# Sorting the value rows of later batches: one full-array matmul per 512 columns, or sixteen 32 by 32 array tiles per 384

## The chip, the cores and the metric

The kernel runs on one core of a Trainium2 chip. The metric is the device time of one execution in microseconds; a profiled execution has in addition a span, from its first to its last instruction, and a trace of every instruction on the five engines: TensorE (PE, with its weight loads as PEld), VectorE (DVE), ScalarE (ACT), GpSimd (POOL) and SyncE (SP), which issues transfers.

## The reference

Attention over blocks that are first mixed by a doubly normalised matrix, and then a two-layer network with a squared relu. The shapes: 4 batches, 8 heads, 768 positions in 8 blocks of 96, head dimension 64; the network goes from 512 to 2048 and back for 3072 tokens.

```python
P = sort_net                                  # (4, 8, 8, 8)
for _ in range(5):
    P = np.exp(P - np.max(P, axis=-1, keepdims=True))
    P = P / (np.sum(P, axis=-1, keepdims=True) + 1e-09)
    P = P / (np.sum(P, axis=-2, keepdims=True) + 1e-09)
k_sorted = np.einsum('bhij,bhjcd->bhicd', P, k_b)
v_sorted = np.einsum('bhij,bhjcd->bhicd', P, v_b)
scores = scale * np.matmul(q_b, k_sb.transpose(0, 1, 2, 4, 3))   # within a block
attn = softmax(scores)
x = np.matmul(attn, v_sb)                     # to (3072, 512)
h = x @ w_in
out = (s * np.maximum(h, 0.0) ** 2 + b) @ w_out
```

## The kernel before

Everything is in bfloat16 with 32-bit sums. A raw tile of keys or values of one batch has 128 partitions and 48 x 64 columns. The partition is (head, block j, half z of the block), and a head is (a, e): pair a of four, member e of two. The column is (c, d): position c in the half block, and head dimension d.

Sorting mixes the blocks of a head: a sum over j. `build_pd` turns a batch's mixing matrix into a 128 by 128 weight `PD[b]` that is zero wherever the heads or the halves differ, so that one matmul over all 128 partitions sorts all heads at once. Its columns are (e, z, a, i), i being the new block.

The work of batch b is written out by hand into slots of the network of the batch before. `ffn1(t, slots)` is the first layer of half batch t: eight times two groups of four matmuls (tile `hps`, line 473), a relu on ScalarE (line 485), a square on VectorE (line 486), and after group i the pieces listed under slot i. `ffn2(t, slots)` is the second layer (tile `ops`, line 497), three output tiles of sixteen matmuls with a store each (`store`, lines 522 and 525), and a slot after every four matmuls. Each engine works through its instructions in the order written.

For b from 1 to 3, with n = b + 1, the loop at the end of the kernel issues the loads of keys and query rows of batch n on the GpSimd queue (`load`, `load_q_rows`), then `ffn1(2b)`, `ffn1(2b + 1)`, `ffn2(2b)` and `ffn2(2b + 1)`. The slots of the first of these, `u0`, sort the values of batch n; those of `ffn2(2b)` sort its keys (`k_pairs`, tile `tpp`); those of `ffn2(2b + 1)` hold its scores (`s_piece`, tile `sc`), products (`p_piece`, tile `pv`), the transposes of its result (`t_dma`) and `build_pd` for the batch after. So the sorting of values that the change touches runs twice, for batches 2 and 3. Batch 1's values go another way (`v_piece`, tile `tv`), batch 0's too.

Values of batches 2 and 3 so far:

- `v_rows(n, u)`, slots 0 to 5: one matmul of 512 columns of the raw tile with `PD[n]` (line 347, tile `tvr`), and a VectorE copy back over the columns that were read (line 349).
- `v_back(n)`, slot 5: the sorted tile has the new block in its partitions, and the products want the position there. So it goes to DRAM in two transfers of 64 partitions on the sync queue (line 354), and back in four (line 358) into `VS`, whose partitions are (z, c) and whose columns are head and block. Each of the four reads what one of the two wrote.
- `q_dma(n)` (QD), slot 5 behind it on the same queue: two transposing transfers of the query rows (line 456).
- `load("v", n + 1, ...)` (LV), where a further batch follows: a one-column copy on GpSimd that waits for the transposed queries (line 90), and six loads (line 93).

The PSUM tiles come from two pools. `psa`, tag "a", has three buffers of two banks, used in turn by `hps`, `sc`, `pv` and the key sorting. `psb`, tag "b", has two buffers of one bank, used in turn by `ops`, `tvr` and others. A tile that takes a buffer waits until the one before it there has been read.

The script's order of the slots before:

```python
u0 = {i: [VRW(n, i)] for i in range(6)}
u0[5] += [VB(n), QD(n)]
```

Of the kernel before, what the change touches and what calls it, by code (L numbers as in the profile page):

```python
# [9 lines left out]
FP = mybir.dt.float32  # L10
BF = mybir.dt.bfloat16
AF = mybir.ActivationFunctionType
ALU = mybir.AluOpType
AX = mybir.AxisListType


def spread(t, dims):

    return bass.AP(tensor=t.tensor, offset=t.offset, ap=[list(t.ap[0])] + dims)
# [3 lines left out]
def kernel(  # L23
# [12 lines left out]
    nc = tc.nc  # L36

    B, H, S, D = q.shape
    NB = sort_net.shape[-1]
    BLK = S // NB  # L40
    BH = B * H
    NHP = H // 2
# [3 lines left out]
    HB = NB // 2  # L46
    TG = HB * BLK
    C2 = BLK // 2
    GAP = 64
    KR = GAP + C2  # L50
    NG = NHP * NB
# [5 lines left out]
    raw = [t.rearrange("b h (j z c) d -> b (h j z) (c d)", j=NB, z=2) for t in (q, k, v)]  # L57

    const = ctx.enter_context(tc.tile_pool(name="const", bufs=1))
# [7 lines left out]
    drp = ctx.enter_context(tc.tile_pool(name="drp", bufs=1, space=bass.MemoryType.DRAM))  # L67
    osb = ctx.enter_context(tc.tile_pool(name="osb", bufs=3))
    psa = ctx.enter_context(tc.tile_pool(name="psa", bufs=3, space=bass.MemoryType.PSUM))
    psb = ctx.enter_context(tc.tile_pool(name="psb", bufs=2, space=bass.MemoryType.PSUM))  # L70
# [9 lines left out]
    for c in range(0, C2, CV):  # L80
        nc.sync.dma_start(out=v0f[:, c:c + CV, :].rearrange("p c d -> p (c d)"),
                          in_=raw[2][0][:, c * D:(c + CV) * D])

    RAW = {}
# [36 lines left out]
    VS = [const.tile([KR, 2 * NG, VW], BF, name=f"vs{i}") for i in range(2)]  # L121
# [63 lines left out]
    nc.vector.memset(eps, 1e-9)  # L185
    jsel = const.tile([128, NB], FP)
    bm = const.tile([128, 2 * 2 * NHP], FP)
    idv = ident.rearrange("p (a e j z) -> p a e j z", a=NHP, e=2, j=NB)

    def permute(eng, b, src, cs=slice(0, C2), ds=slice(0, D)):  # L190
# [15 lines left out]
    def q_banks(b, half, engs):  # L206
# [3 lines left out]
        for u in range(2):  # L210
            tr = psb.tile([128, 1024], BF, tag="b", name="tqb")
            for a in range(2 * u, 2 * u + 2):
                for c in range(CQ):
                    for e in range(2):
# [9 lines left out]
            out=jsel, in_=ident.rearrange("p (h j z) -> p j h z", h=H, j=NB), axis=AX.XY, op=ALU.add),  # L224
        lambda: nc.vector.tensor_reduce(
            out=bm.rearrange("p (e z a) -> p e z a", e=2, z=2),
            in_=idv.rearrange("p a e j z -> p e z a j"), axis=AX.X, op=ALU.add),
# [3 lines left out]
                            op=ALU.subtract)  # L231
# [3 lines left out]
    for it in range(5):  # L235
# [8 lines left out]
        if it == 4:  # L244
            break
        nc.vector.tensor_reduce(out=rstat, in_=sn.rearrange("p i j -> p j i"),
                                axis=AX.X, op=ALU.add)
        if it == 0:
# [2 lines left out]
        nc.vector.tensor_tensor(out=sn, in0=sn, in1=spread(rrec, [[0, NB], list(rrec.ap[1])]),  # L251
                                op=ALU.mult)
    PD = {}
    later = const.tile([128, 2, B // 2, NB * NB], FP)

    def spread_rows(b, o):
# [14 lines left out]
    def build_pd(b, rows):  # L271
        tmp = rtp.tile([128, NB, NB], FP, tag="tmp", name="tmp")
        nc.vector.tensor_tensor(out=tmp, in0=rows.rearrange("p (i j) -> p i j", j=NB),
                                in1=spread(jsel, [[0, NB], list(jsel.ap[1])]), op=ALU.mult)
        pt = rtp.tile([128, NB], FP, tag="pt", name="pt")
        nc.vector.tensor_reduce(out=pt, in_=tmp, axis=AX.X, op=ALU.add)
        cs = rtp.tile([128, 1], FP, tag="cs", name="cs")
        nc.vector.tensor_reduce(out=cs, in_=pt, axis=AX.X, op=ALU.add)
        rc = rtp.tile([128, 1], FP, tag="rc", name="rc")
        nc.vector.reciprocal(out=rc, in_=cs)  # L280
        pd = const.tile([128, 2, 2, NG], BF, name=f"pd{b}")
        nc.vector.scalar_tensor_tensor(
            out=pd.rearrange("p e z (a i) -> p (e z a) i", i=NB),
            in0=spread(bm, [list(bm.ap[1]), [0, NB]]), scalar=rc,
            in1=spread(pt, [[0, 4 * NHP], list(pt.ap[1])]), op0=ALU.mult, op1=ALU.mult)
        PD[b] = pd

    def k_piece(b, c0, eng):
        ps = psa.tile([128, CK, 2, NG], FP, tag="a", name="tp")
# [50 lines left out]
        half(0, eng)  # L340
        return lambda eng: half(1, eng)

    def v_rows(b, u):
        w = 512 // D
        r = RAW["v", b][:, u * w:(u + 1) * w, :].rearrange("p c d -> p (c d)")
        ps = psb.tile([128, 512], FP, tag="b", name="tvr")
        nc.tensor.matmul(out=ps, lhsT=PD[b].rearrange("p e z g -> p (e z g)"), rhs=r,  # L347
                         start=True, stop=True)
        nc.vector.tensor_copy(out=r, in_=ps)  # L349

    def v_back(b):
        vd = drp.tile([2, 2, NG, C2, D], BF, tag="vd", name="vd")
        for e in range(2):
            nc.sync.dma_start(out=vd[e].rearrange("z g c d -> (z g) (c d)"),
                              in_=RAW["v", b][e * 64:(e + 1) * 64].rearrange("p c d -> p (c d)"))
        for e in range(2):
            for z in range(2):
                nc.sync.dma_start(
                    out=VS[b % 2][z * GAP:z * GAP + C2, e * NG:(e + 1) * NG, 0:D],
                    in_=vd[e, z].rearrange("g c d -> c g d"))  # L360

    AT = {}
    X = {}
# [42 lines left out]
        AT[b, half, hp] = at  # L406

    def p_piece(b, half, hp, fill=0):
        g0 = hp * NB + half * HB
        atf = AT.pop((b, half, hp)).rearrange("p e t -> p (e t)")  # L410
        if hp == 0:
            X[b, half] = xp.tile([BLK, HB, d_model], BF, tag="x", name="x")
        x = X[b, half]
        pv = psa.tile([128, 2, 512], FP, tag="a", name="pv")
        for i in range(fill):
            nc.tensor.matmul(out=pv[:, i % 2, 272:512], lhsT=zeros[:, 0:128], rhs=zeros[:, 0:240],  # L416
                             start=True, stop=True)
        for e in range(2):
            for n in range(HB):
                c0 = (e * HB + n) * BLK  # L420
                m = 128 if c0 + 128 <= 2 * TG else BLK
                nc.tensor.matmul(out=pv[0:m, e, n * VW:(n + 1) * VW],  # L422
                                 lhsT=atf[:, c0:c0 + m], rhs=VS[b % 2][:, e * NG + g0 + n, :],
                                 start=True, stop=True)
        pvv = pv[0:BLK, :, 0:HB * VW].rearrange("p e (n w) -> p e n w", w=VW)
        rec = rtp.tile([BLK, 2, HB], FP, tag="rec", name="rec")
        nc.vector.reciprocal(out=rec, in_=pvv[:, :, :, D])  # L427
        nc.vector.tensor_tensor(  # L428
            out=x[:, :, hp * 128:(hp + 1) * 128].rearrange("p n (e d) -> p e n d", e=2),
            in0=pvv[:, :, :, 0:D],  # L430
            in1=rec.unsqueeze(3).broadcast_to([BLK, 2, HB, D]), op=ALU.mult)
# [160 lines left out]
    def SC(b, h, i): return lambda: s_piece(b, h, i)  # L592
    def P(b, h, i): return lambda: p_piece(b, h, i)
    def TP(b, h, i, eng): return lambda: t_piece(b, h, i, eng)
    def VRW(b, u): return lambda: v_rows(b, u)
    def VB(b): return lambda: v_back(b)
    def TD(b, h): return lambda: t_dma(b, h)
    def PDB(b): return lambda: build_pd(b, later[:, b % 2, b // 2, :])
    def QD(b): return lambda: q_dma(b)
    def LV(b): return lambda: load("v", b, 6, QT[b - 1][:, NB - 1, 0, 0:1])  # L600
# [39 lines left out]
    for b in range(1, B):  # L640
        n = b + 1
        s0, s1, u0, u1 = {}, {}, {}, {}
        if n < B:
            load("k", n, 6, XT[2 * b + 1][:, HB - 1, NHP - 1, 0:1])
            load_q_rows(n)
            s0, s1 = halves(n)
            u0 = {i: [VRW(n, i)] for i in range(6)}
            u0[5] += [VB(n), QD(n)]
            if n + 1 < B:
                u0[5] += [LV(n + 1)]  # L650
        ffn1(2 * b, u0)
        ffn1(2 * b + 1, u1)
        ffn2(2 * b, s0)
        ffn2(2 * b + 1, s1)
# [30 lines left out]
```

## Time and profile before

| | before |
|---|---|
| median of 3 runs | 222.98 us (222.55, 222.98, 224.73) |
| profiled execution, its own time | 222.54 us |
| its span | 220.4 us |
| granted TensorE clock | 0.999 |
| PE / DVE / ACT / POOL busy | 213.6 / 126.0 / 109.4 / 70.8 us |
| first layer, line 473 | 512 matmuls |
| second layer, line 497 | 350 matmuls recorded |
| old sorting of values, line 347 | 12 matmuls of 512 columns |

The views used below: the page gives busy times and the share of each engine in the chain that ended last. The chain can also be read in order of time; there a row gives the time that a piece of work holds the chain, which for matmuls that follow one another is their pitch and not the longer duration of a single one. The groups of instructions by line give the mean duration of each shape. The timeline gives single instructions, with what ended the idle time ahead of them in square brackets. Lines with SPq show when the sync queue issues a transfer and how long the issue takes.

### The profile page before, as it was taken

What the parts mean: (1) busy time and instruction counts of PE and PEld (TensorE: products, weight loads), DVE (VectorE), ACT (ScalarE), POOL (GpSimd) and SP (SyncE); (2) the same over time, 40 slices, a digit from 0 to 9 for tenths busy, and PEclk for the clock granted to TensorE, in tenths of its full rate; (3) what the DMA queues carried; (4) which work ended last, traced back from release to release, by engine and by line L of the source; (5) the groups of instructions that cost most, each with busy time, mean ns of one, the idle gap of its engine ahead of it and who ended that gap; (6) DMA issues with size and microseconds to landing.
All of it is one profiled execution on the core that took longest, in us unless ns stands there. A gap on an engine that the chain in (4) does not pass through costs nothing.

```text
span 220.4 us, 5172 instructions
## 1 busy us (share of the span) xinstructions
PE 213.6 (97%) x2156; PEld 128.8 (58%) x2175; DVE 126.0 (57%) x257; ACT 109.4 (50%) x149; POOL 70.8 (32%) x127
## 2 busy tenths in 40 slices
PE   7989999999999999999999999999999999999994
PEld 5877766555465555666446555665446566654454
DVE  6777457567875768547636677547417744441222
ACT  4677687658635445664622535665424356550000
POOL 7659781689832004920050008800000000000000
PEclk9999999999999999999999999999999999999999
DMA  6999999999979662999979846999911940001212
GB/s 154 284 164 125 120 170 204 204 172 134 128 215 181 49 187 41 178 208 121 141 204 175 107 135 88 208 179 102 215 72 48 123 119 3 0 0 48 93 53 95
DMA packets 67255, 28.92 MB, mean 131 GB/s; under 512 B 51872, under 2 KB 63264, under 8 KB 67232
## 3 DMA queue, kind: packets, MB, share of 16 engines
q0 software_dynamic: 31168, 12.85, 49.5%
q1 hardware_dynamic: 36064, 15.74, 35.6%
q8 instruction: 17, 0.28, 0.6%
q14 instruction: 6, 0.05, 0.1%
HBM read 28.85 MB, written 7.86 MB: 167 GB/s over the span
## 4 chain that ended last, share of the span: by engine, by line
PE 90%; DMA 5%; DVE 1%; issue 1%; POOL 1%; ACT 0%; POOLq 0%
PE hps L473 38%; PE ops L497 36%; DMA rawk<-in_k_dram 5%; PE pv L422 4%; PE sc L380 3%; PE tpp L302 2%; PE ops L514 2%; PE tv L328 2%; PE tvr L347 1%; DVE vs L204 1%; PE tr L439 1%; PE scb L398 1%; POOL rawk L93 0%; PE sc L257 0%; PE pv L416 0%
## 5 line engine op out<-in xcount | busy, mean ns | idle before, releaser
L473 PE MATMUL hps<-xt,wi 128*128 128x384 bf16 x512 | 87.9, 326 | 0.0
L497 PE MATMUL ops<-wo,gt 128*128 128x512 bf16 x350 | 82.4, 379 | 1.4 <-issue 0.6
L485 ACT ACTIVATE rt<-hps 128x768 bf16<-128x768 f32 x64 | 51.8, 811 | 39.5 <-PE hps L473 38.3
L473 PEld LDWEIGHTS <-wi 128*128 128x128 bf16 x512 | 49.0, 98 | 32.6 <-issue 0.4
L486 DVE TENSOR_TENSOR gt<-rt 128x768 bf16<-128x768 bf16 x64 | 36.0, 565 | 41.2 <-ACT rt L485 41.0
L497 PEld LDWEIGHTS <-gt 128*128 128x128 bf16 x368 | 34.1, 98 | 37.4
L522 DVE SCALAR_TENSOR_TENSOR ot<-ops,s_bc,bias 128x512 f32<-128x512 f32 (+2 forms) x27 | 18.6, 691 | 34.7 <-PE ops L497 31.6
L388 ACT ACTIVATE at<-sc 112x768 bf16<-112x768 f32 x24 | 18.1, 808 | 30.1 <-PE sc L380 30.1
L428 DVE TENSOR_TENSOR x<-pv,rec 96x512 bf16<-96x512 f32 x32 | 22.0, 686 | 1.1
L115 POOL DMA_DIRECT2D qtok<-in_q_dram x24 | 18.6, 808 | 0.7 <-issue 0.7
L422 PEld LDWEIGHTS <-at 112*128 112x128 bf16 (+1 forms) x256 | 12.9, 101 | 6.7 <-ACT at L388 1.0
L202 ACT CAST ks<-tpp 64x512 bf16<-64x512 f32 x18 | 13.2, 731 | 4.7 <-DVE ks L204 4.1
L140 POOL DMA_DIRECT2D wi<-in_moe_w_in_dram x24 | 12.8, 558 | 5.5 <-DMA rawk<-in_k_dram 3.2
L422 PE MATMUL pv<-vs,at 112*128 112x66 bf16 (+1 forms) x256 | 13.9, 195 | 0.1
L204 DVE CAST ks<-tpp 64x512 bf16<-64x512 f32 x18 | 13.1, 729 | 0.9 <-ACT ks L202 0.5
L93 POOL DMA_DIRECT2D rawk<-in_k_dram x21 | 11.2, 550 | 2.7 <-issue 1.9
L93 POOL DMA_DIRECT2D rawv<-in_v_dram x18 | 9.7, 558 | 6.0 <-DMA wo<-in_moe_w_out_dram 4.6
L130 PE MATMUL z<-zeros 128*64 128x96 bf16 (+2 forms) x129 | 9.8, 241 | 1.3 <-DVE zeros L118 1.2
L90 POOL COPY rawk<-xt 128x1 bf16<-128x1 bf16 x2 | 0.4, 190 | 32.8 <-DMA xt<-x 32.8
L427 DVE RECIPROCAL rec<-pv 96x8 f32<-96x8 f32 x32 | 6.4, 200 | 6.4 <-PE pv L422 6.4
L130 PEld LDWEIGHTS <-zeros 128*64 128x64 bf16 (+1 forms) x130 | 7.5, 115 | 3.0 <-DVE zeros L118 1.2
L349 DVE CAST rawv<-tvr 128x512 bf16<-128x512 f32 x12 | 8.2, 683 | 0.0
(93 smaller groups left out, 137.9 us busy)
## 6 DMA issues: line engine op xcount, KB each, us to landing
out_dram<-ot SPq DMA_DIRECT2D x22, 256.0 KB, 2.6
rawv<-in_v_dram POOLq DMA_DIRECT2D x18, 128.0 KB, 5.3
rawk<-in_k_dram POOLq DMA_DIRECT2D x18, 128.0 KB, 4.1
qtok<-in_q_dram POOLq DMA_DIRECT2D x24, 96.0 KB, 6.5
wo<-in_moe_w_out_dram POOLq DMA_DIRECT2D x4, 512.0 KB, 10.8
v0f<-in_v_dram SPq DMA_DIRECT2D x4, 384.0 KB, 5.9
vd<-rawv SPq DMA_DIRECT2D x4, 384.0 KB, 6.4
vs<-vd SPq DMA_DIRECT2D x8, 192.0 KB, 8.1
```

Of the source, the lines that this page charges most:

```text
L93: nc.gpsimd.dma_start(out=ti[:, c:c + n, :].rearrange("p c d -> p (c d)"), in_=raw["qkv".index(t)][b][:, c * D:(c + n) * D])
L115: nc.gpsimd.dma_start(out=QTOK[b][:, n], in_=qv[:, n])
L130: nc.tensor.matmul(out=z[0:m, 0:w], lhsT=zeros[:, 0:m], rhs=zeros[:, 0:w], start=True, stop=True)
L204: nc.vector.tensor_copy(out=out, in_=in_)
L388: nc.scalar.activation(out=at, in_=sc[0:KR, :, 0:TG], func=AF.Exp, scale=scale)
L422: nc.tensor.matmul(out=pv[0:m, e, n * VW:(n + 1) * VW], lhsT=atf[:, c0:c0 + m], rhs=VS[b % 2][:, e * NG + g0 + n, :], start=True, stop=True)
L428: nc.vector.tensor_tensor(out=x[:, :, hp * 128:(hp + 1) * 128].rearrange("p n (e d) -> p e n d", e=2), in0=pvv[:, :, :, 0:D], in1=rec.unsq ...
L473: nc.tensor.matmul(out=H1[t, i][:, f, 0:TG], lhsT=wi[:, hp, fc:fc + 128], rhs=XT[t][:, :, hp, :], start=(hp == 0), stop=(hp == NHP - 1))
L485: nc.scalar.activation(out=rt, in_=h, func=AF.Relu)
L486: nc.vector.tensor_tensor(out=gt[:, 2 * i:2 * i + 2, :], in0=rt, in1=rt, op=ALU.mult)
L497: nc.tensor.matmul(out=ops, lhsT=gt[:, f, m * 128:(m + 1) * 128], rhs=wo[:, f, :], start=(f == 0), stop=(f == NF - 1))
L522: nc.vector.scalar_tensor_tensor(out=ot[:, ns], in0=ops, scalar=s_bc, in1=BIAS[0][:, ns], op0=ALU.mult, op1=ALU.add)
```

## The change

The sum over j stays within a head, and with (a, e, j, z) as the partition a head pair is 32 partitions. The changed kernel builds for batches 2 and 3 a second weight `PW[b]` with only 32 columns (z, e, i) beside `PD[b]`, from a mask `bmz` that is made once. A pair's 32 rows are one row group of the array.

`v_tiles(b, r)` takes the place of three `v_rows`. It has two rounds, r = 0 and 1, in slots 0 and 2. The raw tile's 3072 columns are eight stretches of 384, and round r takes the stretches 2c + r. For each c from 0 to 3 and each pair a there is one matmul of 32 rows and 32 columns: row group a, column group c, 384 columns of data, into PSUM bank a, partitions 32c onward. The four banks are one "a" tile and both "b" tiles. VectorE copies two banks at once and one more by itself, and ScalarE copies one.

The sorted tile now has (c, z, e, i) in its partitions and (a, r, x) in its columns. `v_back` sends it to DRAM in four transfers of 32 partitions and reads it back in two, one for each z. In `VS` the order of blocks and pairs changes, which `p_piece` follows in its index. `VB`, `QD` and `LV` move from slot 5 to slot 2.

```diff
+    bmz = const.tile([128, 2 * 2], FP)
...
         PD[b] = pd
+        if b >= 2:
+            if b == 2:
+                nc.vector.tensor_reduce(out=bmz.rearrange("p (z e) -> p z e", z=2),
+                                        in_=bm.rearrange("p (e z a) -> p z e a", e=2, z=2),
+                                        axis=AX.X, op=ALU.add)
+            pw = const.tile([128, 2 * 2 * NB], BF, name=f"pw{b}")
+            nc.vector.scalar_tensor_tensor(
+                out=pw.rearrange("p (x i) -> p x i", i=NB),
+                in0=spread(bmz, [list(bmz.ap[1]), [0, NB]]), scalar=rc,
+                in1=spread(pt, [[0, 4], list(pt.ap[1])]), op0=ALU.mult, op1=ALU.mult)
+            PW[b] = pw
...
-    def v_rows(b, u):
...
+    NC = C2 // 8
+
+    def v_tiles(b, r):
+        w = NC * D
+        raw = RAW["v", b].rearrange("p c d -> p (c d)")
+        two = psa.tile([128, 2, 512], FP, tag="a", name="tvr")
+        one = [psb.tile([128, 512], FP, tag="b", name="tvs") for _ in range(2)]
+        bank = [two[:, 0], two[:, 1], one[0], one[1]]
+        for c in range(4):
+            for a in range(NHP):
+                pr = slice(a * 32, (a + 1) * 32)
+                c0 = (2 * c + r) * w
+                nc.tensor.matmul(out=bank[a][c * 32:(c + 1) * 32, 0:w], lhsT=PW[b][pr, :],
+                                 rhs=raw[pr, c0:c0 + w], start=True, stop=True,
+                                 tile_position=(a * 32, c * 32))
+        v4 = raw.rearrange("p (a r x) -> p a r x", a=NHP, r=2)
+        nc.vector.tensor_copy(out=v4[:, 0:2, r], in_=two[:, :, 0:w])
+        nc.scalar.copy(out=v4[:, 2, r], in_=one[0][:, 0:w])
+        nc.vector.tensor_copy(out=v4[:, 3, r], in_=one[1][:, 0:w])

     def v_back(b):
-        vd = drp.tile([2, 2, NG, C2, D], BF, tag="vd", name="vd")
-        for e in range(2):
...
+        w = 2 * NC * D
+        vd = drp.tile([2 * 2 * NB, NHP, 4, w], BF, tag="vd", name="vd")
+        for c in range(4):
+            nc.sync.dma_start(out=vd[:, :, c],
+                              in_=RAW["v", b][c * 32:(c + 1) * 32].rearrange(
+                                  "p (a x) d -> p a (x d)", a=NHP))
+        for z in range(2):
+            nc.sync.dma_start(
+                out=VS[b % 2][z * GAP:z * GAP + C2, :, 0:D],
+                in_=vd[z * 2 * NB:(z + 1) * 2 * NB].rearrange("i a c (y d) -> (c y) (i a) d", d=D))
...
-        g0 = hp * NB + half * HB
+        def g(n):
+            i = half * HB + n
+            return i * NHP + hp if b in PW else hp * NB + i
...
-            u0 = {i: [VRW(n, i)] for i in range(6)}
-            u0[5] += [VB(n), QD(n)]
+            u0 = {0: [VT(n, 0)], 2: [VT(n, 1), VB(n), QD(n)]}
             if n + 1 < B:
-                u0[5] += [LV(n + 1)]
+                u0[2] += [LV(n + 1)]
```

More of the change, by code (lines that the diff above doesn't have):

```diff
@@ L253 @@
     PD = {}
+    PW = {}
     later = const.tile([128, 2, B // 2, NB * NB], FP)
@@ L286, in build_pd @@
         PD[b] = pd
+        if b >= 2:
+            if b == 2:
+                nc.vector.tensor_reduce(out=bmz.rearrange("p (z e) -> p z e", z=2), in_=bm.rearrange("p (e z a) -> p z e a", e=2, z=2),
+                                        axis=AX.X, op=ALU.add)
[5 more added lines that the diff above has]
+            PW[b] = pw
     def k_piece(b, c0, eng):
@@ L341, in v_piece @@
         return lambda eng: half(1, eng)
-    def v_rows(b, u):
[L344 to L349, printed above, removed]
-    def v_back(b):
-        vd = drp.tile([2, 2, NG, C2, D], BF, tag="vd", name="vd")
-        for e in range(2):
[L354 to L360, printed above, removed]
+    NC = C2 // 8
@@ L422, in p_piece @@
                 nc.tensor.matmul(out=pv[0:m, e, n * VW:(n + 1) * VW],
-                                 lhsT=atf[:, c0:c0 + m], rhs=VS[b % 2][:, e * NG + g0 + n, :],
+                                 lhsT=atf[:, c0:c0 + m], rhs=VS[b % 2][:, e * NG + g(n), :],
                                  start=True, stop=True)
@@ L594, in TP, with VT @@
     def TP(b, h, i, eng): return lambda: t_piece(b, h, i, eng)
-    def VRW(b, u): return lambda: v_rows(b, u)
+    def VT(b, r): return lambda: v_tiles(b, r)
     def VB(b): return lambda: v_back(b)
```

## The prediction

> **What bounds the kernel now.** I read the page first: which engine fills the span, which engine the chain that ended last runs through, and whether the matmul clock is full.
>
> ```profile
> PE 213.6 (97%) x2156; PEld 128.8 (58%) x2175; DVE 126.0 (57%) x257; ACT 109.4 (50%) x149; POOL 70.8 (32%) x127
> PEclk9999999999999999999999999999999999999999
> PE 90%; DMA 5%; DVE 1%; issue 1%; POOL 1%; ACT 0%; POOLq 0%
> ```
>
> TensorE (PE) is busy for 97% of the span, carries 90% of the chain, and its clock is full throughout. So a change matters through the time it gives TensorE or takes from it, or through a wait that it puts in front of a matmul. The second view is the chain in order of time around the code that changes, for batch 2, whose value rows are sorted during the first input layer of batch 1 (columns: start us, us, what; the DMA in the page's chain is its first row here, long before the change).
>
> ```profile
> 3.18 11.13 DMA rawk<-in_k_dram
> ...
> 78.87 1.30 PE hps L473 x8
> 80.17 0.22 PE tvr L347
> 80.39 1.30 PE hps L473 x8
> 81.69 0.22 PE tvr L347
> ...
> 87.75 0.22 PE tvr L347
> ```
>
> Here TensorE never waits. Eight matmuls of the input layer take 1.30 us, then one sorting matmul of 512 columns stands in the chain with 0.22 us. From 80.17 to 80.39 and from 81.69 to 81.90, by the next slot's start, it is 0.217 us, six times: 1.30 us a batch. Batch 3 does the same (twelve such matmuls in all), so 2.60 us of the chain belong to the old sorting. That is the most that could be won.
>
> **The change, part by part.**
>
> *Matmuls on the chain.* Removed: 12 matmuls of 512 columns, 2.60 us. Added: four rounds (two for each of batches 2 and 3) of 16 matmuls, each on a 32 by 32 piece of the array with 384 columns. No row shows such a piece, but the chain has smaller splits, each an excursion from full-array work and back:
>
> ```profile
> 26.10 0.88 PE tqb L216 x48
> 28.70 0.28 PE scb L398 x8
> 45.09 0.98 PE cps L576 x16
> 60.04 1.64 PE tv L328 x96
> 64.38 0.62 PE tv L328 x32
> 113.53 0.45 PE sc L380 x16
> 175.92 20.80 PE hps L473 x128
> ```
>
> hps is whole-array: 20.80 / 128 = 162.5 ns for 384 columns, so 384 columns at 2.4 a ns (160 ns) and 2.5 ns beside. The two tv rows differ by 64 matmuls and 1.02 us: 15.9 ns for 64 columns, where a lone one would need 64 / 2.4 + 2.5 = 29.2 ns. The pieces of 64 array columns therefore run two at a time (14.6 ns) with little lost. What is left, 1.64 - 96 x 15.9 = 0.11 us, is the price of leaving the full array and coming back. cps has four pieces of 32 array columns and 512 columns of data: 16 x (213.3 + 2.5) / 4 = 0.86 us, and 0.98 was measured: again 0.12 over. sc has two row halves: eight more matmuls cost 0.45 - 0.28 = 0.17 us, or 21 ns each, where two at a time gives (40 + 2.5) / 2 = 21.3; over: 0.11. So a round costs 0.115 us plus its matmuls divided by how many run at once. Four column pieces are shown, two row pieces too; both axes together by four are not.
>
> With all 16 at once the stream lasts 162.5 ns, and the round 0.28 us if they start together: the lower bound. The upper bound takes the closest spacing of starts that any row shows, 15.9 ns: 15 x 15.9 + 162.5 + 115 = 0.52 us. That spacing is already explained by the streaming of pairs, so the true spacing should be smaller; I take the middle, 0.40 us. Four rounds: 1.60 us (1.12 to 2.06). Against 2.60 us the gain is **1.0 us** (0.54 to 1.48).
>
> The Trainium skill speaks to this on both sides. "TensorE: Matmul & The Clock Gate", Part 3, gives about 4 ns between the starts of packed pieces; an estimate by that page is 60 + 162.5 + 115 = 0.34 us a round, a gain of 1.25 us. The same page, under "Wait — 56ns, not 53.3ns?", says starts never come closer than about 25 ns; the tv rows with 15.9 ns contradict it for pieces of 64 columns, yet if it held for 32 by 32 pieces it would cancel the change (first rival).
>
> *Evacuation.* Removed: 12 VectorE copies. Added per round: a VectorE copy of 768 columns, one of 384, and a ScalarE copy of 384. The rows for VectorE (L204) and ScalarE (L202) on PSUM tiles, columns as in the costliest groups:
>
> ```profile
> L204 DVE CAST ks<-tp 128x1024 bf16<-128x1024 f32 x1 | 1.2, 1223 | 0.3 <-PE tp L292 0.3
> L204 DVE CAST ks<-tkb 128x512 bf16<-128x512 f32 x1 | 0.7, 681 | 0.0
> L202 ACT CAST ks<-tp 128x1024 bf16<-128x1024 f32 x1 | 1.0, 1013 | 0.3 <-PE tp L292 0.3
> L202 ACT CAST ks<-tkb 128x512 bf16<-128x512 f32 x1 | 0.6, 592 | 0.0
> L349 DVE CAST rawv<-tvr 128x512 bf16<-128x512 f32 x12 | 8.2, 683 | 0.0
> 80.21 0.81 ACT L485 ACTIVATE rt<-hps 128x768 bf16<-128x768 f32 x1 [2.27 <-PE hps L473]
> 81.05 0.56 DVE L486 TENSOR_TENSOR gt<-rt 128x768 bf16<-128x768 bf16 x1 [0.83 <-ACT rt L485]
> 81.72 0.81 ACT L485 ACTIVATE rt<-hps 128x768 bf16<-128x768 f32 x1 [0.70 <-PE hps L473]
> ```
>
> Interpolated: 0.95 us for 768 columns on VectorE (0.68 to 1.22), 0.55 for 384 (0 to 0.68), 0.49 on ScalarE (0 to 0.59). Per batch VectorE does 2 x 1.5 = 3.0 us in place of 6 x 0.68 = 4.1. ScalarE's new 0.49 us fits in the 0.70 us for which it waits for the next hps. What could reach TensorE is the buffer of the second round. The first round runs 80.17 to 80.57; the relu ends at 81.02 and its square on VectorE at 81.61; the wide copy ends at 82.57 and the narrow one at 83.15. TensorE does two hps groups from 80.57 and asks for the same three buffers at 83.17. The last is free 0.02 us before, so it fits by a hair: a semaphore's delay may hold the fourth matmul a few hundredths of a us, which I cost at nothing, as it lies inside the bounds of the round. If the wide copy took 1.22 us, the second round would wait 0.27 us, 0.54 for both batches (a rival). The input layer's third, fourth and sixth groups also take turns in the larger buffers: the sixth starts at 86.17 and its buffer is free at about 85.6.
>
> *The extra weights.* For batches 2 and 3 VectorE builds a second, smaller matrix (128 x 32) behind the first, and once a mask by a reduction.
>
> ```profile
> L225 DVE TENSOR_REDUCE bm<-ident 128x16 f32<-128x128 bf16 x1 | 0.3, 266 | 0.0
> 65.12 0.35 DVE L282 SCALAR_TENSOR_TENSOR pd<-bm,rc,pt 128x128 bf16<-128x128 f32 x1
> 68.19 0.75 DVE L522 SCALAR_TENSOR_TENSOR ot<-ops,s_bc,bias 128x512 f32<-128x512 f32 x1 [2.72 <-PE ops L497]
> ```
>
> At most 0.35 + 0.27 = 0.62 us, in front of 2.72 us in which VectorE waits for TensorE: nothing. Without that cover it would be 0.62 once and 0.35 once.
>
> *The way to DRAM and back, and what moves with it.* The stores, the transposed load of the queries and the next value load move from the sixth slot to the third. First the sync queue, then the rows that consume (start, us), then the transfers' sizes and times to landing:
>
> ```profile
> 89.86 1.15 SPq L354 DMA_DIRECT2D vd<-rawv  x2
> 95.47 8.86 SPq L358 DMA_DIRECT2D vs<-vd  x4
> 104.55 4.91 SPq L456 DMA_TRANSPOSE qt<-qtok  x2
> SPq L354 <- DVE rawv L349: 8.1, 1, 8.1
> 112.17 0.19 POOL L90 COPY rawv<-qt 128x1 bf16<-128x1 bf16 x1 [17.02 <-DMA qt<-qtok]
> 113.46 0.51 PE L380 MATMUL sc<-qt,ks 64*128 64x96 bf16 x16
> 116.51 0.43 PE L422 MATMUL pv<-vs,at 112*128 112x66 bf16 x8
> vd<-rawv SPq DMA_DIRECT2D x4, 384.0 KB, 6.4
> vs<-vd SPq DMA_DIRECT2D x8, 192.0 KB, 8.1
> qtok<-in_q_dram POOLq DMA_DIRECT2D x24, 96.0 KB, 6.5
> ```
>
> The queue waits 8.1 us for the last copy and stores at 89.86. In the new order the second round's copies end near 86.2, so the stores start 3.6 us earlier. Four stores instead of two cost two more issues of about 0.57 us (1.15 / 2). Bytes and the 128-byte pieces of the way back stay; two transfers carry what four did. One thing is worse: each of the old four loads needed one store, each new one needs all four. If the stores land 6.4 us after the last issue at about 87.9, the loads begin near 94.3, before the 95.47 of now, and the transposes follow about a us sooner than 104.55. Behind them on the sync queue stand only the output stores of the second layer; on POOL the next value load waits for the transposes, and nothing urgent is behind it. The transposes have all landed by 112.17 and scores begin at 113.46: 1.29 us of slack. The last value load is issued before 104.33 (95.47 + 8.86) and needs 8.1 us; its first consumer runs at 116.51: some 4 us of slack. I cost the move at nothing. Without the cover, a delay beyond 1.3 us goes on the path one for one.
>
> **Sum.** -2.60 + 1.60 = -1.0 us. The profiled execution took 222.54 us (span 220.4 us), equal to the fastest of the three runs (222.55); their median is 222.98. The same 1.0 us gives 221.5 on the profiled execution and **222.0** on the median, 0.45% faster. 1% is 2.2 us, about what a measurement of this kernel can tell from no change.
>
> **The rivals.**
>
> A. *Issue-bound rounds.* Starts 25 ns apart make a round 15 x 25 + 162.5 + 115 = 0.65 us, just the three 0.217 us that it replaces: **223.0**. For it: 16 separate weight loads and matmuls instead of three. Against it: the tv rows with 15.9 ns.
>
> B. *The pieces queue along one axis.* If the row groups or the column groups don't overlap fully, the round is 0.115 + 16 x 0.1625 / W, with W at once. It decides at W below 4.9, where the round passes 0.65 us. At W = 4 it is 0.765 us, four rounds lose 0.46 us: **223.4**, slower than before. At W = 2 it is 1.415 us, 3.06 us lost: **226.0**; at W = 1, 231.2. For it: only one axis at a time is shown in this trace, and row groups by two at most. Against it: cps reaches four and sc two with nothing lost.
>
> C. *The query transposes come late.* Place: the sync queue, held in front of the value loads until all four stores land. If each small store took as long as one of the old (95.47 - 89.86 = 5.6 us for the first, about 8 us for both, so 4 us each), four would end near 86.2 + 16 = 102.2, and the transposes would end 4 to 7 us later than now: less the 1.3 us of slack, 2.7 us or more for batch 2 and something like it for batch 3. Less the 1.0 won: **226.5**. Against it: each new store has half the bytes, and starts while fewer transfers run.
>
> D. *The second round waits for VectorE*, 0.27 us in each batch, 0.54 in all: a gain of 0.46, **222.5**. It is the tightest spot, but the interpolated copy just avoids it.
>
> **How the numbers follow.** Forecast 0.68; A 0.10; D 0.05; B at W = 4 0.06; B at W = 2 or less 0.06; C 0.05. The forecast's own bounds, from the median, are 222.98 - 1.48 = 221.5 and 222.4. The runs shown spread from 222.55 to 224.73, and the profiled execution lies 0.44 us under the median, so 221.1 is the lower end. Above, the range takes in A and B at W = 4 with a margin of 0.2: 223.6. Left out are B at W = 2 and C, 0.11. Faster by over 1% needs more than 2.2 us of the 2.60, a round below 0.1 us, which one 384-column stream already exceeds; only scatter could show it: 0.04. Slower by over 1%: B at W = 2 or less and C: 0.11. Within 1%: 0.85.
>
> **What would show it right or wrong.** In the chain the six rows of 0.22 us give way to two of 0.3 to 0.5 us in each batch, after the first and third hps groups; 0.7 or more speaks for B, 0.65 for A. A gap before the second of them with VectorE as releaser is D. ScalarE has four copies near 0.49 us, VectorE four near 0.95 and four near 0.55. The first store's issue should stand near 86 and the transposes at or before 104; if scores wait for the transposes, it is C. The forecast is wrong if the rounds are below 0.28 or above 0.52 us, or if a wait shows in front of any matmul after them.

## The result and the profile after

The changed kernel takes 221.71 us (median of 20 runs), the kernel before 222.78 us (20 runs beside it). The ratio is 0.995, 95% interval 0.9937 to 0.9964: 1.07 us less, 0.5%; the interval allows 0.8 to 1.4 us. The profiled execution's span is 219.6 us against 220.4. Ratios, here and below, are of fast executions alone, which leaves out a single one: 226.25 us, with the query rows loaded first.

The page first. TensorE remains the bound.

```profile
PE 213.2 (97%) x2208; PEld 128.5 (59%) x2227; DVE 123.8 (56%) x256; ACT 110.8 (50%) x153; POOL 71.3 (32%) x127
```

The chain in order of time around the change, kernel after. The six rows of 0.22 us are gone; two short visits to the small tiles stand there, and nothing waits.

```profile
79.09 1.30 PE hps L501 x8
80.39 0.26 PE tvr L367 x2
...
80.70 2.71 PE hps L501 x16
83.41 0.26 PE tvr L367 x2
...
83.72 17.00 PE hps L501 x104
...
127.08 1.30 PE hps L501 x8
...
131.71 17.01 PE hps L501 x104
...
175.06 20.80 PE hps L501 x128
```

The same marks in the kernel before:

```profile
87.97 13.00 PE hps L473 x80
...
127.40 1.30 PE hps L473 x8
...
136.49 13.00 PE hps L473 x80
```

Stage by stage, from the first hps group to the end of the last one: before 78.87 to 100.97 (22.10 us), after 79.09 to 100.72 (21.63). For the next batch 127.40 to 149.49 (22.09) against 127.08 to 148.72 (21.64). So the two stages with sorting lose 0.47 and 0.45 us. The second layers between lose 0.07 (100.97 to 127.40 against 100.72 to 127.08) and 0.09 us. The sum is 1.08 us. In the span 0.22 us of it are lost again, as the first stage shown begins that much later in this execution. The delay is older than the change: the input layer's 24 matmuls behind `cps` begin at 46.28 instead of 46.06 us, and the first changed instruction, the mask, runs on VectorE at 65.60.

**What a round costs.** The chain puts 0.31 us to a visit (80.39 to 80.70), but the stage lost only 0.47 us: its 128 hps matmuls need 128 x 162.5 ns = 20.80 us, and 21.63 - 20.80 = 0.83 us is left for two rounds, 0.415 each. The missing 0.10 hides in the next row: sixteen hps matmuls take 2.71 us there, where sixteen whole-array pitches are 2.60. The timeline of TensorE shows why (start us, us, engine, line, operation, shapes).

```profile
80.06 0.33 PE L501 MATMUL hps<-xt,wi 128*128 128x384 bf16 x1
80.32 0.33 PE L367 MATMUL tvr<-rawv,pw 32*32 32x384 bf16 x2
...
80.36 0.33 PE L367 MATMUL tvs<-rawv,pw 32*32 32x384 bf16 x2
80.63 0.34 PE L501 MATMUL hps<-xt,wi 128*128 128x384 bf16 x1
```

Starts are safer than modelled ends. The first small piece starts 0.26 us after the last hps matmul, 0.10 more than a pitch: the way in. All sixteen starts fall within 0.04 us. The next hps matmul starts 0.27 us after the last small piece, 0.11 more than a stream of 384 columns: the way back. In all 0.10 + 0.04 + 0.16 + 0.11 = 0.41 us. (The chain has the same pieces 0.07 us later, since it counts from the modelled end of the matmul before.)

What the 0.10 and 0.11 us are is open. The weight loads of the same stretch fit two readings:

```profile
78.88 1.12 PEld L501 LDWEIGHTS <-wi 128*128 128x128 bf16 x8
80.32 0.14 PEld L367 LDWEIGHTS <-pw 32*32 32x32 bf16 x16 [0.32 <-issue]
80.63 2.39 PEld L501 LDWEIGHTS <-wi 128*128 128x128 bf16 x16 [0.17 <-DVE x L456]
```

Among full-array matmuls the weights come ahead: the eighth load has ended at 80.00, and its matmul starts at 80.06. On the way in and on the way back the first load starts together with its matmul, at 80.32 and at 80.63. So TensorE may have to empty itself at the change, or the weights, 98 ns for a full-array load, may merely not be loaded ahead there. No run tells the two apart; what is shown is that each visit pays both losses.

**Evacuation**, groups by shape, kernel after (busy us, mean ns):

```profile
L371 DVE CAST rawv<-tvr 128x768 bf16<-128x768 f32 x4 | 3.8, 950 | 0.0
L373 DVE CAST rawv<-tvs 128x384 bf16<-128x384 f32 x4 | 2.2, 548 | 0.0
L372 ACT CAST rawv<-tvs 128x384 bf16<-128x384 f32 x4 | 1.9, 472 | 0.0
```

**The transfers**, sync queue of the kernel after, with the first scores of batch 2:

```profile
86.31 3.20 SPq L379 DMA_DIRECT2D vd<-rawv  x4
96.37 5.82 SPq L383 DMA_DIRECT2D vs<-vd  x2
102.37 10.36 SPq L484 DMA_TRANSPOSE qt<-qtok  x2
113.23 0.52 PE L405 MATMUL sc<-qt,ks 64*128 64x96 bf16 x16
```

The first of the two transposes alone, as the trace answers for the stretch in which it is issued: time to landing, after and before.

```profile
DMA to landing us min/median/max: 10.7/10.7/10.7
```

```profile
DMA to landing us min/median/max: 5.8/5.8/5.8
```

The stores start 3.6 us earlier than before, the loads 0.9 us later. The two loads need 10.8 and 15.0 us to land, so the second, issued at 96.8, lands near 111.8. The first transpose, issued 2.2 us earlier, lands at 102.37 + 10.7 = 113.07: 2.7 us later than before (104.55 + 5.8), and 0.16 us ahead of the scores that read it. The gain was kept by a narrow margin. The second transpose has landed when the value load that waits for it goes on:

```profile
115.30 0.19 POOL L90 COPY rawv<-qt 128x1 bf16<-128x1 bf16 x1 [17.47 <-DMA qt<-qtok]
```

That is 3.1 us later than before (112.17) and behind the first scores, which do not wait for it: `q_dma` brings the new blocks 0 to 3 by its first transpose, and these are all that the first scores read.

### The profile page after: what moved, and what is told of

It reads as the page before. It is cut to its first block, busy times and chain, and to the rows that moved or that the text cites. A ratio compares the mean times of both kernels' runs of the same rounds, so it can differ in the third digit from the quotient of the medians.

```text
span 219.6 us, 5281 instructions
## 1 busy us (share of the span) xinstructions
PE 213.2 (97%) x2208; PEld 128.5 (59%) x2227; DVE 123.8 (56%) x256; ACT 110.8 (50%) x153; POOL 71.3 (32%) x127
## 4 chain that ended last, share of the span: by engine, by line
PE 96%; DVE 2%; issue 1%; ACT 0%
PE hps L501 38%; PE ops L525 36%; PE z L130 5%; PE pv L450 4%; PE sc L405 3%; PE tpp L314 2%; PE ops L542 2%; PE tv L340 2%; DVE vs L205 1%; PE tr L467 1%; PE scb L423 1%; PE tp L304 1%; PE tvr L367 1%; PE sc L259 0%; PE pv L444 0%
## 5 line engine op out<-in xcount | busy, mean ns | idle before, releaser
L501 PE MATMUL hps<-xt,wi 128*128 128x384 bf16 x512 | 86.6, 326 | 0.0
L514 DVE TENSOR_TENSOR gt<-rt 128x768 bf16<-128x768 bf16 x64 | 35.5, 557 | 42.5 <-ACT rt L513 42.4
L130 PE MATMUL z<-zeros 128*64 128x96 bf16 (+2 forms) x129 | 10.6, 254 | 1.3 <-DVE zeros L118 1.2
L90 POOL COPY rawk<-xt 128x1 bf16<-128x1 bf16 x2 | 1.0, 488 | 29.4 <-DMA xt<-x 29.4
L130 PEld LDWEIGHTS <-zeros 128*64 128x64 bf16 (+1 forms) x130 | 8.3, 126 | 3.0 <-DVE zeros L118 1.2
```

The lines of the kernel that those rows point to most:

```text
L130: nc.tensor.matmul(out=z[0:m, 0:w], lhsT=zeros[:, 0:m], rhs=zeros[:, 0:w], start=True, stop=True)
L501: nc.tensor.matmul(out=H1[t, i][:, f, 0:TG], lhsT=wi[:, hp, fc:fc + 128], rhs=XT[t][:, :, hp, :], start=(hp == 0), stop=(hp == NHP - 1))
L514: nc.vector.tensor_tensor(out=gt[:, 2 * i:2 * i + 2, :], in0=rt, in1=rt, op=ALU.mult)
```

## Experiments

Theory T is the account above: all sixteen pieces run at once, and a visit to the small tiles costs 0.10 us in and 0.11 back besides its stream. The first four runs are about the round, the next three about the other parts of the change, the last five about the transfers. The changed kernel's 221.71 us is the measure where nothing else is said; each ratio is to the kernel before on the same chip.

**The loops exchanged.**

```diff
-        for c in range(4):
-            for a in range(NHP):
+        for a in range(NHP):
+            for c in range(4):
```

> The same rounds with the two loops exchanged: the four column groups of one row group follow each other, then the next row group. Theory T (a round of the changed kernel costs about 0.42 us: 0.10 into the small tiles, 0.04 for sixteen starts, 0.16 for one stream of 384 columns, 0.11 back to the full array; all sixteen run at once): the order does not matter, the starts stay 3 to 4 ns apart, 221.7 us. Theory Q (the pieces of a row group queue for its data, and the original order hides that by alternating): starts in groups 0.16 us apart, a round of 0.8 to 0.9 us, 1.6 to 2 us more, about 223.5 us.

Measured: 221.57 us, ratio 0.9922 (0.9891 to 0.9953). Chain:

```profile
80.46 0.28 PE tvr L367 x8
...
80.77 2.71 PE hps L501 x16
83.48 0.28 PE tvr L367 x8
```

0.31 us a visit and 3.02 us from visit to visit, as in the changed kernel (80.39 to 83.41). The pieces of a row group do not queue. Q falls for this order.

**Every round twice.**

```diff
-        for c in range(4):
+        for c in [c for _ in range(2) for c in range(4)]:
```

> Every round issues its sixteen matmuls twice in a row, the second time with the same result into the same place. Theory T: the second sixteen add one more stream and their starts, 0.16 to 0.20 us a round, no second way in or back: 0.65 to 0.8 us more than the changed kernel, 222.4 us. Theory S (no cost of switching; each small piece costs 0.42 / 16 = 26 ns of issue): 0.42 us a round more, 1.7 us in all, 223.4 us. Theory Q (four at once): 0.65 us a round, 2.6 us in all, 224.3 us.

Measured: 222.01 us, ratio 0.9943 (0.992 to 0.9966); span 220.2 us. Chain, the second sixteen beginning at 80.47:

```profile
80.16 0.26 PE tvr L367 x2
...
80.47 0.12 PE tvr L367 x2
...
80.63 2.71 PE hps L501 x16
83.34 0.27 PE tvr L367 x2
```

Sixteen more pieces add 0.16 us (80.47 to 80.63): one stream of 384 columns, no more. Visit to visit is 3.18 us instead of 3.02, and the two stages last 21.96 us each instead of 21.63 and 21.64, so the four rounds cost 0.65 us more. The span shows 0.6. The time alone could not tell: the ratio is 0.9943 here, 0.995 in the changed kernel and 0.9922 with the loops exchanged. S would have 1.7 us and Q 2.6, more than chain or time show: both are out. The pieces do run sixteen at a time, and the rest of the 0.41 us is paid once a visit.

**Each round in two visits.**

```diff
-        for c in range(4):
+        for c in range(2 * part, 2 * part + 2):
...
-            u0 = {0: [VT(n, 0)], 2: [VT(n, 1), VB(n), QD(n)]}
+            u0 = {0: [VT(n, 0, 0)], 1: [VT(n, 0, 1)],
+                  3: [VT(n, 1, 0)], 4: [VT(n, 1, 1), VB(n), QD(n)]}
```

> Each round in two halves of eight pieces, in two neighbouring slots with a group of the input layer between: eight short visits to the small tiles in place of four, with as many pieces in all. The stores and what follows them move to slot 4. Theory T: a visit costs 0.10 + 0.02 + 0.16 + 0.11 = 0.39 us, eight cost 3.1 us where four cost 1.7: 1.4 us more than the changed kernel, 223.1 us, the whole gain gone. Theory S: as many pieces, so the same time, 221.7 us.

Measured: 222.81 us, ratio 0.999 (0.9967 to 1.0012): the gain is gone with as many pieces and as much data. Chain:

```profile
80.10 0.26 PE tvr L372 x2
...
80.39 1.41 PE hps L508 x8
81.79 0.26 PE tvr L372 x2
```

From visit to visit 1.69 us, less 1.30 for eight hps: 0.39 us for eight pieces, where sixteen cost 0.41. Again the way back is in the hps row, 1.41 instead of 1.30. The two stages last 22.36 and 22.37 us, 1.46 in all above those of the changed kernel, as Theory T has it (1.4); the time rose by 1.1.

**The second round one slot earlier.**

```diff
-            u0 = {0: [VT(n, 0)], 2: [VT(n, 1), VB(n), QD(n)]}
+            u0 = {0: [VT(n, 0)], 1: [VT(n, 1), VB(n), QD(n)]}
```

> The second round comes one group of the input layer after the first, not two (slots 0 and 1). Theory T with the cover as told in the prediction: the fourth matmul of the second round asks for a PSUM bank near 82.0 us in the trace of the changed kernel, and VectorE has read it at 83.16 us. So TensorE stands for about 1.2 us in each of the two batches: 2.4 us more, 224.1 us. Rival: the banks are free in time anyway, as ScalarE and VectorE keep up: no change, 221.7 us.

Measured: 223.82 us, ratio 1.0032 (1.0007 to 1.0057), 2.1 us more than the changed kernel. Timeline:

```profile
83.17 0.33 PE L367 MATMUL tvr<-rawv,pw 32*32 32x384 bf16 x2
83.18 0.33 PE L367 MATMUL tvs<-rawv,pw 32*32 32x384 bf16 x1
83.75 0.55 DVE L373 CAST rawv<-tvs 128x384 bf16<-128x384 f32 x1
84.35 0.32 PE L367 MATMUL tvs<-rawv,pw 32*32 32x384 bf16 x1 [0.84 <-DVE rawv L373]
```

Three pieces start, the fourth comes 1.17 us later, when VectorE has emptied its bank. The group of the input layer between the rounds is what hides the evacuation, and one group does not hide it: the prediction's rival D, made real. The second batch has the same gap (132.33 to 133.50).

**Stores and what follows back in slot 5.**

```diff
-            u0 = {0: [VT(n, 0)], 2: [VT(n, 1), VB(n), QD(n)]}
+            u0 = {0: [VT(n, 0)], 2: [VT(n, 1)], 5: [VB(n), QD(n)]}
```

> The changed kernel with the stores, the query transposes and the next value load back in slot 5; the rounds stay in slots 0 and 2. In the trace of the changed kernel the stores were issued at 86.3 us, but the loads only at 96.4 and the last query transpose landed at 115.3, three us later than before. Theory M (the move is worth nothing, since the transfers wait for one another and for the key and query loads): the same time within 0.3%, with the loads issued at 97 to 99 us. Theory C (the transposes have become tight: scores begin at 113.2 us): the queries land after 113.2 us, TensorE waits 1 to 3 us in front of the scores of batch 2, 222.7 to 224.7 us.

Measured: 221.43 us, ratio 0.9936 (0.9923 to 0.9949). Sync queue:

```profile
86.44 3.23 SPq L379 DMA_DIRECT2D vd<-rawv  x4
96.15 5.87 SPq L383 DMA_DIRECT2D vs<-vd  x2
```

Nothing moved. SyncE is a queue of its own: it issues when the copies are done, in whichever slot of TensorE's order the instruction is written. (Between the two slots nothing else is put on the sync queue.) This part of the change does nothing; the early copies do.

**Four stores and two loads alone**, in the kernel before.

```diff
-            nc.sync.dma_start(out=vd[e]..., in_=RAW["v", b][e * 64:(e + 1) * 64]...)
+            for z in range(2):
+                p0 = e * 64 + z * 32
+                nc.sync.dma_start(out=vd[z, e]..., in_=RAW["v", b][p0:p0 + 32]...)
...
-                    in_=vd[e, z].rearrange("g c d -> c g d"))
+                in_=vd[z].rearrange("e g c d -> c (e g) d"))
```

> The kernel before with the changed shape of the transfers alone: four stores of 32 partitions and two loads, each of which needs all its two stores, in slot 5; the sorting itself is as before. Theory M: no time changes (0 within 0.3% of the kernel before), and the last transpose lands later than 112.2 us. Rival: the smaller stores alone give or cost time, 0.3 us or more.

Measured: 222.92 us against 222.79, ratio 1.0006 (0.9991 to 1.0021): no effect on the time. The value load that waits for the last transpose:

```profile
113.68 0.19 POOL L90 COPY rawv<-qt 128x1 bf16<-128x1 bf16 x1 [17.66 <-DMA qt<-qtok]
```

1.5 us later than the 112.17 of before, in an execution whose stage began 0.2 us later. The first transpose is issued at 104.44 us and needs 7.2 us, so it lands 2.0 us ahead of the first scores (113.64), against 3.1 before (110.35 and 113.46): in this one trace the shape of the transfers alone takes part of the slack.

**The order of columns alone**, in the kernel before, by a second 128 by 128 weight.

```diff
+            for x in range(4):
+                nc.vector.scalar_tensor_tensor(
+                    out=px.rearrange("p e z (i a) -> p (e z) i a", a=NHP)[:, x], ...)
...
-                                 rhs=VS[b % 2][:, e * NG + g0 + n, :],
+                                 rhs=VS[b % 2][:, e * NG + g(n), :],
```

> The kernel before with the changed order of blocks and pairs in the sorted values alone (block outer, pair inner), made by a second full-size weight. In the changed kernel a group of eight product matmuls held the chain for 0.26 us, in the one before for 0.27 us; sixteen such groups after the first batch are 0.1 to 0.2 us of the gain. Theory O (the order of columns does it): 0.26 us in this kernel's chain too, and 0.1 to 0.2 us faster than before. Rival (scatter of the records): 0.27 us, and the same time as before.

Measured: 222.32 us against 222.79, ratio 0.9991 (0.9969 to 1.0013). Chain, this kernel, and after it the kernel before:

```profile
117.03 0.26 PE pv L434 x8
```

```profile
116.67 0.27 PE pv L422 x8
```

The second layers of this kernel, between the end of one input layer and the start of the next:

```profile
101.32 0.86 PE ops L509 x4
127.67 1.30 PE hps L485 x8
```

They last 26.35 and 26.34 us here, 26.43 twice in the kernel before, 26.36 and 26.34 in the changed one. So the order of columns, with nothing else changed in the products, gives the whole 0.07 and 0.09 us of the second layers. This is shown in the chain. In the time it is not: the medians differ by 0.47 us, more than the 0.1 to 0.2 expected, and the interval of the ratio includes no change.

**The transfers.** Four runs on one chip: the changed kernel again, query rows loaded first, the rounds in slots 3 and 5, four loads.

> The changed kernel itself, on the chip of the three runs beside it: 221.7 us, a ratio near 0.995 to the kernel before; in its trace the first query transpose of batch 2 lands within 1 us of the first scores (102.4 + 10.7 = 113.1 against 113.2 us in the trace seen so far).

> The changed kernel with the loads of the query rows ahead of those of the keys on the GpSimd queue, behind the first half's transposed result, so that they run while the transfers are nearly idle. Theory L (the transposes land so close to the scores that in some executions TensorE waits for them): the first transpose of batch 2 lands 2 us or more ahead of the scores, the slowest executions go, the median is 0.2 to 0.5 us below that of the changed kernel. Theory M (0.1 us of slack is still slack): the transposes land earlier and the time stays within 0.15 us.

```diff
+            QTOK[n] = rawp.tile([BLK, NB, H, D], BF, tag="rawq", name="qtok")
+            nc.gpsimd.tensor_copy(out=QTOK[n][:, 0, 0, 0:1],
+                                  in_=XT[2 * b][0:BLK, HB - 1, NHP - 1, 0:1])
+            load_q_rows(n)
             load("k", n, 6, XT[2 * b + 1][:, HB - 1, NHP - 1, 0:1])
-            load_q_rows(n)
```

> The changed kernel with its rounds in slots 3 and 5, so that the sorted values are ready when they were in the kernel before, near 90 us, and the stores start there. Theory L: the transfers behind them come as much later, the first transpose of batch 2 lands up to 3 us after TensorE could begin the scores, and the kernel takes 1 to 3 us more than the changed one: 222.7 to 224.7 us. Theory M (the transposes end with the whole queue of transfers, which begins with the key loads and not with the stores): they land where they do now, no change, 221.7 us.

```diff
-            u0 = {0: [VT(n, 0)], 2: [VT(n, 1), VB(n), QD(n)]}
+            u0 = {3: [VT(n, 0)], 5: [VT(n, 1), VB(n), QD(n)]}
```

> The changed kernel with its two loads of 384 KB split into four of 192 KB, each still behind all four stores. If the size of the loads delays the transposes behind them (landing 10.7 us after issue, against 5.8 us in the kernel before), the first one lands 2 to 4 us earlier; if it is the start of the loads at 96.4 us and the bytes in the queue, it lands within 1 us of where it does now. The time: 221.7 us in both cases, or 0.2 to 0.5 us less if the transposes held up some executions.

```diff
-        for z in range(2):
+        for x in range(4):
+            z, e = x // 2, x % 2
             nc.sync.dma_start(
-                out=VS[b % 2][z * GAP:z * GAP + C2, :, 0:D],
-                in_=vd[z * 2 * NB:(z + 1) * 2 * NB].rearrange(...))
+                out=VS[b % 2][z * GAP:z * GAP + C2, e * NG:(e + 1) * NG, 0:D],
+                in_=vd[x * NB:(x + 1) * NB].rearrange(...))
```

| | time, us | ratio to before | first transpose lands, us | first scores, us |
|---|---|---|---|---|
| changed kernel again | 221.93 | 0.9976 (0.9933 to 1.0018) | 113.9 | 114.05 |
| query rows first | 221.45 | 0.9933 (0.9911 to 0.9955) | 109.5 | 113.53 |
| rounds in slots 3 and 5 | 221.47 | 0.9931 (0.9916 to 0.9945) | 113.7 | 113.78 |
| four loads | 221.90 | 0.9948 (0.9935 to 0.9961) | 111.4 | 113.45 |

In two of the four traces the scores do wait. The changed kernel again, timeline:

```profile
104.08 9.54 SPq L484 DMA_TRANSPOSE qt<-qtok  x2
114.05 0.52 PE L405 MATMUL sc<-qt,ks 64*128 64x96 bf16 x16 [0.26 <-DMA qt<-qtok]
114.02 0.40 PEld L405 LDWEIGHTS <-ks 64*128 64x128 bf16 x16 [0.72 <-issue]
```

In the trace of the changed kernel shown above TensorE loaded no weights for 0.42 us ahead of the scores; here for 0.72, so 0.30 us are lost, and with the rounds in slots 3 and 5 it is 0.91, so 0.49. That is rival C at a small size, in some executions. With the rounds in slots 3 and 5 the stores start at 90.26 us, four later, and the transpose lands only 0.6 us later than in the first trace (113.65 against 113.07): the end of this run of transfers hardly depends on the start of the stores. Theory L's 1 to 3 us is wrong. With four loads the queue gets to the transposes later (106.37 us instead of 104.08), and the first then needs 5.0 us instead of 9.8: it lands 2.5 us earlier and has 2 us of slack. Query rows first gives 4 us.

Of these two only the second is clear of the scatter. In batch 2 the first transpose lands at 112.8, 110.95 and 113.1 us in the runs with the loops exchanged, with every round twice and with the stores in slot 5, whose transfers are those of the changed kernel; so four loads, at 111.4, lie within what two can give, and query rows first, at 109.5, does not. In batch 3 four loads land it at 159.1 us, and two at 159.3 to 161.2 in seven traces. (Query rows first stands apart here too, at 157.3.)

The four intervals overlap, so none of this can be told in the time. The longest wait, with the rounds in slots 3 and 5, goes with a time as short as that with the query rows first. Nor did the slowest executions go with the wait, as Theory L had said they would: two of six took 224.04 and 224.60 us in the changed kernel again, and two of six 222.69 and 226.25 us with the query rows first.

Both remedies together:

> The changed kernel with both ways to bring the query transposes forward: query rows loaded ahead of the keys, and four loads of the sorted values in place of two. Theory L (the transposes hold up the scores of batch 2 by 0.3 to 0.5 us in some executions of the changed kernel): the first transpose lands 3 us or more ahead of the scores, no wait in front of them, 221.3 to 221.5 us and no execution of the undisturbed kind above 222.0. Theory M (what separates the variants is scatter): the same trace, but 221.5 to 221.9 us.

Measured: 221.47 us, ratio 0.9942 (0.9925 to 0.996), one of six runs above 222.0 (222.25). Sync queue and weight loads:

```profile
100.53 6.87 SPq L485 DMA_TRANSPOSE qt<-qtok  x2
113.03 0.37 PEld L406 LDWEIGHTS <-ks 64*128 64x128 bf16 x16 [0.42 <-issue]
```

The first transpose needs 8.6 us and lands at 109.1, almost 4 us ahead of the scores, and no wait is left. Theory L's bound on the slowest execution did not hold. The ratio lies within the interval of the changed kernel's. By this trace it is the version with the most room, not a measurably faster one.

## Why the prediction was right, point by point

**The bound** was read rightly: what TensorE saved in the two stages, 0.92 us, and 0.16 in the second layers, came out of the time. The 0.16 is a term that the prediction does not have: it counted no gain from the order of columns. So its 1.0 us stands against 0.92 where it looked for it.

**The size of a round** was right in sum, 0.40 predicted and 0.41 measured, from two terms that were both off and cancelled. The price of a visit was taken as 0.115 us for leaving and returning. The rows of tv, cps and sc from which it came end where the last piece ends, so 0.115 is the way in alone. The way back is in the row that follows, as the hps row of 2.71 us shows. The trace of before had it too, in the row behind cps:

```profile
46.06 4.01 PE hps L473 x24
```

Twenty-four pitches of 162.5 ns are 3.90 us, so 0.11 is left for the way back. Both together are 0.21. The other term is the spacing of starts: I allowed 0 to 0.24 us for sixteen starts and took the middle, and it is 0.04. That the two errors cancelled is luck. With both terms right the sum would have been 2.60 - 1.64 = 0.96 us, by reasons that hold.

The figure of about 4 ns between starts in the Trainium skill ("TensorE: Matmul & The Clock Gate", Part 3) agrees with this trace, 0.04 us over sixteen. The floor of about 25 ns between starts in the Trainium skill ("TensorE: Matmul & The Clock Gate", "Wait — 56ns, not 53.3ns?") does not hold for these pieces: rival A is out by the starts at 80.32 to 80.36. The Trainium skill, "TensorEngine Tiling (Array Packing)", Key Properties, says that a change of tiling mode drains the engine; the 0.21 us of a visit here fit that, but no run here tells a drain from a weight load that does not come ahead.

**Rival B** (queueing along one axis) is out by the doubled rounds: 0.16 us for sixteen more.

**Evacuation**: the three copies were interpolated at 0.95, 0.55 and 0.49 us and measured 0.950, 0.548 and 0.472. Rival D did not come: the narrow copy ends at 83.16 us (82.61 + 0.55), and the fourth matmul of the second round starts at 83.34. That is 0.18 us to spare, where 0.02 had been worked out; the run with neighbouring slots shows what happens when it is missed.

**The extra weights** cost nothing, as said: 0.16 us for the mask and 0.25 for the smaller matrix, and the wait of VectorE behind them is 2.35 us instead of 2.72.

**The move** was the weak step. The start of the stores was right, and by the right reason: the copies were to end near 86.2 us, and the stores were issued at 86.31. That they stand in an earlier slot as well does nothing, as the run with slot 5 shows. Two other things failed. It said that the loads would begin near 94.3 us and the transposes be issued about a us sooner than before. The last of the four stores was issued at 88.93 us instead of 87.9 and needed 7.3 us instead of 6.4, so the loads began at 96.37. The transposes were issued 2.2 us sooner, but the first, behind larger loads, needed 10.7 us instead of 5.8. The run with two loads alone has 7.2; where the rest comes from is open.

And the slack was read from the wrong transfer. The 1.29 us are from the landing of the last transpose to the first scores, which need only the first one. For that one the slack was 3.11 us (110.35 to 113.46); it shrank to 0.16 in one execution and was overdrawn by 0.30 in another. By the prediction's own rule, one for one beyond 1.3 us, the last transpose, 3.1 us later than before, would have cost 1.8 us. That it cost nothing is luck of the same kind: two errors that cancelled.

So rival C was given too large a size, but the direction and the place were right. (Its price was not added up rightly either: twice 2.7 us less 1.0 gives 227.4, not 226.5.) By the prediction's last sign, no wait in front of any matmul after the rounds, the trace shown first passes, and those of the changed kernel again and of slots 3 and 5 do not. Costing the move at nothing was near enough for the median; it was not free of risk.

## What to carry to other kernels

A short visit to small array tiles in the midst of full-array work costs its way in and its way back before anything is won: here 0.21 us beside 0.16 of stream. So bundle the pieces into as few visits as PSUM allows; halving the bundles ate the whole gain. Give the evacuation of one visit enough other matmuls before the next: here two groups of 1.30 us covered it and one did not.

The stores' place among TensorE's slots did not matter here, only their place on their own queue and the data they wait for. Before moving one, ask what data it waits for and what ends last behind it, and measure slack from the landing of the very transfer that the next step reads: an earlier issue was eaten here by a longer wait in the transfers.

When the price of an excursion is read from a chain, add the row after it: the loss on returning is booked there.

## What was not expected of the hardware

Sixteen 32 by 32 pieces start within 0.04 us, and a second sixteen into the same banks follow without any gap (0.16 us for 16 x 384 columns). The first DMA transpose of batch 2 needed between 5.0 and 13.3 us from issue to landing with the same bytes in the loads ahead of it: behind four loads 5.1 and 5.8 in kernels with the old sorting, 5.0 and 8.6 with the new; behind two loads 7.2 with the old sorting, and 8.0 to 13.3 in the nine traces with the new. What else than the loads decides this is open. Eight matmuls with 66 columns took 0.26 us with one order of their columns in the source tile and 0.27 with another, which alone makes 0.07 to 0.09 us in each second layer; why is open, as only the order was tried.
